# Attention, dense FFN and top-2 MoE on one core: paired score products, a whole fp32 spill, gates first, and late weight conversions

## The chip, the core and the metric

The kernel runs on one core of a Trainium2 chip. Its engines are TensorE (PE in the rows, with PEld for its weight loads), VectorE (DVE), ScalarE (ACT), GpSimd (POOL) and the queue of SyncE (SP), which here only issues transfers; transfers are also issued from POOL. Every instruction stream runs in its own order and waits on semaphores. The metric is the device time of one execution in microseconds, the median of three runs.

## The reference, cut to what is computed

```python
def _attn_ref(q, k, v, f):                       # B 4, H 8, S 576, D 64
    scores = scale * np.matmul(q, k.transpose(0, 1, 3, 2))
    cum = np.cumsum(np.log(np.clip(f, 0.0001, 1.0)), axis=-1)
    decay = cum[:, :, :, None] - cum[:, :, None, :]
    scores = np.where(causal, -1000000000.0, scores + decay)
    scores = scores - np.max(scores, axis=-1, keepdims=True)
    attn = np.exp(scores)
    attn = attn / (np.sum(attn, axis=-1, keepdims=True) + 1e-09)
    return np.matmul(attn, v)
def _moe_ref(x, w_in, w_out):                    # 2304 x 512, d_ff 2048
    h = np.maximum(x @ w_in, 0.0)
    return h * h @ w_out
def _moe2_ref(x, w_gate, w_noise, noise, w1, w2):   # 8 experts, 512 x 1024
    noisy_logits = x @ w_gate + np.log1p(np.exp(x @ w_noise)) * noise
    top2 = ...                                   # two experts a token, softmax of the two
    for e in range(E):
        for k in range(2):
            mask = top2[:, k] == e
            h = np.maximum(x[mask] @ w1[e], 0.0)
            out[mask] += top2_w[mask, k, None] * (h @ w2[e])
```

The three stages follow one another: attention, a dense feed-forward with a squared ReLU, a mixture of eight experts.

## The kernel before, in words

**Arithmetic.** The large products run in float16. A number is kept as a high and a low half, and a product is three matmuls (high by high, high by low, low by high). So each raw float32 weight block `w` of the dense stage (16 blocks, each with a part of w_in and of w_out) must be split once: DVE L550, L555 and L559 make the high half and the rest, ACT L562 and DVE L565 write the two float16 halves. The raw blocks stand in two buffers of the tag "w64"; the last eight are loaded from POOL's queue (L541), and a load waits until the conversion of the block two before it has let its buffer go.

**Attention.** The first 256 positions of each head, the "heads" part, are cut into 12 sub-steps `j`. `hd_s` (L385 on) makes the scores of one sub-step: two PSUM banks, one for each half `z` of 64 partitions; for each half eight float32 products of hraw (L398), two or four products that add the decay (`c`, L403), and two or four that add the causal mask (L409). DVE takes the row maxima (`smh`, L420), ACT the exponentials (`pr`, L431). Sub-steps 0 to 7 stand in an order written out by hand (`PLAN`), with the first weight loads and conversions; sub-steps 8 to 11 run between the steps of the dense stage, in an order that a list scheduler finds. The other 320 positions (`att_*`; scores L226 to L243, products with v L320 and L323) run later, also between steps of the dense stage, from tiles `setk` and `setq` that are prepared from `qkr` loads. The fixed rows of four `setq` tiles are written by POOL (L178 to L180).

**Dense stage.** The tokens go in six chunks of 384. Step `i` of a chunk multiplies with weight block `i`: `mm1` (L585, `m`), ACT and DVE make `r` and `g` (L592 to L603), `mm2` adds into three PSUM tiles `acc` (L647). Chunks 0 and 1 go in two passes of eight blocks each; between them `spill` writes `acc` to memory as two float16 halves (ACT L625, DVE L626), and `unspill` loads them as `bk`, which PE adds to the second pass by twelve products with `ident2k` (L645). `x2_out` writes a finished chunk: `x2`, its transpose `x2T` and its rows `x2d`.

**Experts.** `router` (DVE L728 to L770: `lg` to `mprev`) and `slots` (to `si`, L792) give each token its places in `table`, which POOL writes by scatters (L795). `slot_rows` reads a part of it back (`tix`, L860, and `gs`); `gather` fetches token rows by it (`xg`, L871) and transposes them (`xgT`, SP, L873). `layer1` (L913) and `layer2` (L930) are the two products of an expert, with `hT` between them (ACT L917, DVE L918); POOL adds the result to the output by a scatter (L934). The float32 weights of the experts come through five buffers `wr` (SP, L812 and L816; `fetch_next`), and `split_next` turns one into float16 halves (ACT L835, DVE L836); eight of these make an expert. While chunk 5 runs, the tables of chunk 4 are finished and the rows of expert 0 are gathered.

## Time and profile before

| what | value |
|---|---|
| median of 3 runs | 978.59 us (976.27 to 986.29) |
| profiled execution | 981.3 us, its span 979.1 us |
| PE busy | 944.0 us, 96% of the span |
| DVE, ACT, POOL busy | 570.3, 445.6, 209.4 us |
| mean granted TensorE clock | 0.983 |

The span is the time from the first to the last record of the profiled execution; 2.2 us lie around it. PE is busy nearly all the time, so what can be won is either work that PE does or the few stretches where it waits or runs at the lower clock. The chain that ended last has 71% of its time on PE, 8% on transfers and 5% on DVE.

### The profile page before, as it was taken

To read this page: it belongs to the slowest core of one execution; us is meant where nothing else is said; L and a number is where in the kernel's file an instruction comes from. 1 tells how busy PE (TensorE), PEld (TensorE's weight loads), DVE (VectorE), ACT (ScalarE), POOL (GpSimd) and SP (SyncE) were. 2 spreads that over 40 slices of the span, in tenths; PEclk is the share of its full clock that TensorE was granted. 3 is DMA by queue.
4 is the path that set the end of the run, shared out by engine and by line. 5 is a ranking of instruction groups with operands and counts; after the bars stand their busy time and mean duration, and the time that the engine had idled before them with its cause. 6 is when DMAs were issued, how large, how long until landed. Compare 5 with 4: busy or idle time off the path is not lost.

```text
span 979.1 us, 17623 instructions
## 1 busy us (share of the span) xinstructions
PE 944.0 (96%) x6866; PEld 547.8 (56%) x6866; DVE 570.3 (58%) x1253; ACT 445.6 (46%) x990; POOL 209.4 (21%) x249
## 2 busy tenths in 40 slices
PE   6899989999999999999999899999999999999996
PEld 5766544554555555555555344657474756565662
DVE  6878888777787788776485241525252534334220
ACT  4775758767486566645473110414141323222110
POOL 2000141014041032011002316232232323111102
PEclk7999999999999999999999899999999999999998
DMA  7367858997979949746493914597958484941303
GB/s 301 118 242 224 200 149 267 176 215 172 224 156 250 204 89 234 144 55 99 106 332 113 210 37 97 106 219 174 241 144 188 129 194 96 236 82 27 42 12 43
DMA packets 219879, 155.34 MB, mean 159 GB/s; under 512 B 175698, under 2 KB 186322, under 8 KB 217746
## 3 DMA queue, kind: packets, MB, share of 16 engines
q1 hardware_dynamic: 207234, 124.75, 51.6%
q0 software_dynamic: 12416, 29.31, 14.3%
q8 instruction: 55, 0.90, 0.4%
q10 hardware_dynamic: 144, 0.13, 0.1%
q14 instruction: 30, 0.25, 0.1%
HBM read 89.05 MB, written 23.98 MB: 115 GB/s over the span
## 4 chain that ended last, share of the span: by engine, by line
PE 71%; DMA 8%; issue 7%; DVE 5%; POOL 3%; ACT 2%; SPq 2%; POOLq 0%; DVEq 0%; ACTq 0%
PE e L913 18%; PE e L930 17%; PE m L585 13%; PE acc L647 12%; PE po L320 2%; SPq L873 1%; DMA wr<-in_w_dram 1%; DMA w<-in_w_io_dram 1%; POOL table L795 1%; PE psab L398 1%; PE ps L226 1%; PE ps L227 1%; DMA pt<-phl 1%; PE po L323 1%; DMA xg<-x2d,tix 1%
## 5 line engine op out<-in xcount | busy, mean ns | idle before, releaser
L930 PE MATMUL e<-w2s,hT 128*128 128x512 f16 (+1 forms) x960 | 211.1, 382 | 2.0 <-ACT hT L917 1.3
L913 PE MATMUL e<-xgT,w1s 128*128 128x310 f16 (+2 forms) x1536 | 207.7, 297 | 4.1 <-DMA xgT<-xg 4.1
L647 PE MATMUL acc<-w,g 128*128 128x512 f16 x864 | 205.4, 380 | 0.0
L913 PEld LDWEIGHTS <-w1s 128*128 128x128 f16 x1536 | 140.3, 98 | 70.3 <-issue 8.2
L585 PE MATMUL m<-xT,w 128*128 128x384 f16 x960 | 173.7, 331 | 4.9 <-ACT r L592 3.7
L917 ACT ACTIVATE hT<-e 128x310 f16<-128x310 f32 (+2 forms) x128 | 54.7, 428 | 268.2 <-PE e L913 267.9
L930 PEld LDWEIGHTS <-hT 128*128 128x128 f16 (+1 forms) x960 | 99.8, 104 | 110.1 <-issue 2.2
L585 PEld LDWEIGHTS <-w 128*128 128x128 f16 x1152 | 109.9, 99 | 81.0 <-issue 10.4
L647 PEld LDWEIGHTS <-g 128*128 128x128 f16 x864 | 81.0, 98 | 86.2 <-DVE g L603 0.3
L933 DVE TENSOR_SCALAR y<-e,gs 128x512 f32<-128x512 f32 (+1 forms) x40 | 30.0, 750 | 159.3 <-PE e L930 133.8
L918 DVE SCALAR_TENSOR_TENSOR hT<-e,hT 128x310 f16<-128x310 f32 (+2 forms) x128 | 60.6, 477 | 80.7 <-ACT hT L917 80.4
L934 POOL DMA_INDIRECT out_dram<-y,tix x40 | 65.0, 1625 | 169.6 <-DVE y L933 125.1
L795 POOL DMA_INDIRECT table<-ent,si x36 | 41.4, 1149 | 166.0 <-DVE si L792 156.6
L592 ACT ACTIVATE r<-m 128x384 f32<-128x384 f32 x80 | 39.2, 490 | 68.1 <-PE m L585 67.7
L255 DVE TENSOR_REDUCE sm<-ps 128x1 f32<-128x384 f32 (+2 forms) x96 | 53.1, 562 | 22.1 <-PE ps L243 8.7
L871 POOL DMA_INDIRECT xg<-x2d,tix x40 | 44.3, 1108 | 83.6 <-DMA xgT<-xg 73.3
L258 ACT ACTIVATE pr<-ps,sm 128x384 f32<-128x384 f32 (+1 forms) x64 | 40.2, 630 | 25.8 <-DVE sm L257 23.4
L593 ACT ACTIVATE g<-r 128x384 f16<-128x384 f32 x96 | 50.1, 521 | 3.2 <-PE acc L647 1.5
L836 DVE SCALAR_TENSOR_TENSOR w2s<-wr,w2s 128x1024 f16<-128x1024 f32 x32 | 39.1, 1223 | 19.8 <-ACT w2s L835 19.8
L602 DVE TENSOR_TENSOR r<-r 128x384 f32<-128x384 f32 x64 | 35.4, 553 | 25.2 <-ACT g L593 24.9
L836 DVE SCALAR_TENSOR_TENSOR w1s<-wr,w1s 128x1024 f16<-128x1024 f32 x32 | 39.0, 1225 | 12.7 <-ACT w1s L835 12.5
L279 DVE TENSOR_TENSOR phl<-pr,phl 128x384 f16<-128x384 f32 (+1 forms) x64 | 38.5, 619 | 13.2 <-ACT phl L278 12.8
(281 smaller groups left out, 1085.2 us busy)
## 6 DMA issues: line engine op xcount, KB each, us to landing
wr<-in_w_dram SPq DMA_DIRECT2D x64, 512.0 KB, 5.2
qkr<-in_qk_dram SPq DMA_DIRECT2D x16, 896.0 KB, 6.0
w<-in_w_io_dram SPq DMA_DIRECT2D x8, 1024.0 KB, 4.8
w<-in_w_io_dram POOLq DMA_DIRECT2D x8, 1024.0 KB, 5.7
vr<-in_v_dram SPq DMA_DIRECT2D x16, 320.0 KB, 4.5
x2d<-x SPq DMA_DIRECT2D x18, 256.0 KB, 2.7
hraw<-in_qka_dram SPq DMA_DIRECT2D x8, 512.0 KB, 5.9
out_dram<-zero SPq DMA_DIRECT2D x5, 768.0 KB, 5.2
```

Of the source, the lines that this page charges most:

```text
L255: seen[u] = nc.vector.tensor_reduce(sm[:, z:z + 1], ps[z][:, :N], AX.X, ALU.max).ins
L585: nc.tensor.matmul(ps, W[i][:, wi, 0, 128 * cc:128 * cc + 128], xT[:, xi, cc, r0:r0 + CH], start=(x == 0), stop=(x == 11))
L593: nc.scalar.activation(g[:, 0, :], r, AF.Square, scale=2.0 ** -10)
L647: last[0] = nc.tensor.matmul(acc[t], g[:, gi, 128 * t:128 * t + 128], W[i][:, wi, 1, :], start=(i in ends[c][0] and x == 0), stop=(i in en ...
L795: s_ = nc.gpsimd.indirect_dma_start(out=table, out_offset=bass.IndirectOffsetOnAxis(ap=si[:, t, k:k + 1], axis=0), in_=ent[:, t, k, :], in ...
L836: nc.vector.scalar_tensor_tensor(lo, t_, sc, hi, op0=ALU.mult, op1=ALU.subtract)
L871: nc.gpsimd.indirect_dma_start(out=xg, out_offset=None, in_=x2d[0:seen, :], in_offset=bass.IndirectOffsetOnAxis(ap=rows_t[key, j][0], axis=0))
L913: last[0] = nc.tensor.matmul(ps[:, :hw], w1s[:, cc, wi, 128 * i:128 * i + 128], xgT[:, 4 * xi + cc, c], start=(x == 0), stop=(x == 11)).ins
L917: relu[0] = nc.scalar.activation(hi, ps[:, :hw], AF.Relu).ins
L918: nc.vector.scalar_tensor_tensor(hT[:, i, 1, c], ps[:, :hw], 0.0, hi, op0=ALU.max, op1=ALU.subtract)
L930: last[0] = nc.tensor.matmul(ps[:m], hT[:, i, hi, 128 * j:128 * j + m], w2s[:, i, wi, :], start=(i == 0 and x == 0), stop=(i == NFE - 1 an ...
L934: s_ = nc.gpsimd.indirect_dma_start(out=out, out_offset=bass.IndirectOffsetOnAxis(ap=ix[:m], axis=0), in_=y[:m], in_offset=None, compute_o ...
```

## The change

1. Nine products on a tile of ones stand first on PE (`NWARM`). The load of the gates `fch` is issued from SP as its first transfer, and no longer from ACT.
2. `ident2k` goes. The fixed rows of three of the four `setq` tiles (`make_q`) are written by POOL among the constants at the start.
3. The last block of keys in the 64-row part (`i` of 4) is multiplied with all 128 rows and not with 64; the mask product likewise.
4. `hd_s` issues its products in the order half 0, half 1, half 0, and so on, and for `j` of 8 and more the scheduler may not change that.
5. `spill` writes one float32 sum (ACT alone). `unspill` is one transfer into a buffer of the tag "w64". The twelve products with `ident2k` go; `x2_out` of chunks 0 and 1 adds `bk` on DVE.
6. The first five `wr` loads may be issued only behind the last `x2d` of chunk 4. Of the 16 splits before the experts, eight run in chunk 5, their DVE half behind `si` (L802 in the changed kernel); the other eight run in `layer1` of expert 0, one for each step.
7. `tix` and `gs` have eight buffers and not six.

```diff
-    fch = chain_load(0, HEAD, "pt", 3, nc.scalar)
+    fch = chain_load(0, HEAD, "pt", 3, nc.sync)
+    busy = consts.tile([128, 1], F16, name="busy")
+    nc.vector.memset(busy, 1.0)
+    pw = psX.tile([128, 512], F32, name="pw", tag="xf", bufs=1)
+    for _ in range(NWARM):
+        nc.tensor.matmul(pw, busy.to_broadcast([128, 128]), busy.to_broadcast([128, 512]), start=True, stop=True)
...
+        prev = None
+        for o_, l_, r_, first, end in prods:
+            with ExitStack() as guard:
+                if j >= NPL and prev is not None:
+                    guard.enter_context(tc.issue_after(prev))
+                prev = nc.tensor.matmul(o_, l_, r_, start=first, stop=end, skip_group_check=True).ins
...
-            sp = gpool.tile([128, 2 * DM], F16, name="sp", tag="x2", bufs=3)
-            nc.scalar.activation(sp[:, :DM], acc[t], AF.Copy, scale=2.0 ** -11)
-            nc.vector.scalar_tensor_tensor(sp[:, DM:], acc[t], 2.0 ** -11, sp[:, :DM], op0=ALU.mult, op1=ALU.subtract)
+            sp = gpool.tile([128, DM], F32, name="sp", tag="x2", bufs=3)
+            nc.scalar.activation(sp, acc[t], AF.Copy)
...
+        back[c] = astream.tile([128, NT, DM], F32, name="bk", tag="w64", bufs=2)
+        nc.sync.dma_start(back[c], part[CH * c:CH * c + CH, :].rearrange("(t p) d -> p t d", p=128))
...
-            if i == NA + 4 and c < 2:
-                for z in range(2):
-                    nc.tensor.matmul(acc[t], ident2k, back[t][:, DM * z:DM * z + DM], start=False, stop=False)
...
+            if c < 2:
+                src = back[c][:, t]
+                nc.vector.tensor_tensor(src, acc[t], src, op=ALU.add)
...
-        tix = epool.tile([128, NJ, 2], I32, name="tix", bufs=6)
+        tix = epool.tile([128, NJ, 2], I32, name="tix", bufs=8)
...
+            for n in (0, 1, 3):
+                make_q(n)
...
-            for _ in range(WR):
-                fetch_next()
-        if c == NCH - 1 and i >= 4:
-            split_next()
+            with tc.issue_after(x2_put[0]):
+                for _ in range(WR):
+                    fetch_next()
+        if c == NCH - 1 and 4 <= i < 12:
+            split_next(slotted[0])
...
-    while at["split"] < 16:
-        split_next()
+    def begin(i):
+        split_next(relu[0])
```

How the streams stand. Lines of the changed kernel are some ten higher than those of the kernel before (L385 to L409 there are L392 to L421 here, L550 to L565 are L561 to L576, L812 and L816 are L822 and L826, L860 is L870, L873 is L883).

DVE, kernel before, around the first spill: `w_964` and `w_1073` are the raw and the new tile of weight block 11, `w_991` and `w_1155` those of block 12, `sp` the halves of the spill.

```order
L550 TENSOR_SCALAR w_1073<-w_964 128x1024
L601 TENSOR_TENSOR g<-r,g 128x384
L421 TENSOR_SCALAR smh<-smh 128x2x2
L555 SCALAR_TENSOR_TENSOR w_1073<-w_964,w_1073 128x1024
L420 TENSOR_REDUCE smh<-psab 128x2
L626 SCALAR_TENSOR_TENSOR sp<-acc_699,sp 128x512
L559 SCALAR_TENSOR_TENSOR w_964<-w_964,w_1073 128x1024
L626 SCALAR_TENSOR_TENSOR sp<-acc_703,sp 128x512
L626 SCALAR_TENSOR_TENSOR sp<-acc_707,sp 128x512
L550 TENSOR_SCALAR w_1155<-w_991 128x1024
```

DVE, changed kernel, the same place: the raw tiles of blocks 11 and 12 are `w_983` and `w_1010`.

```order
L561 TENSOR_SCALAR w_1089<-w_983 128x1024
L612 TENSOR_TENSOR g<-r,g 128x384
L566 SCALAR_TENSOR_TENSOR w_1089<-w_983,w_1089 128x1024
L431 TENSOR_REDUCE smh<-psab 128x2 x2
L570 SCALAR_TENSOR_TENSOR w_983<-w_983,w_1089 128x1024
L432 TENSOR_SCALAR smh<-smh 128x2x2
L561 TENSOR_SCALAR w_1171<-w_1010 128x1024
L566 SCALAR_TENSOR_TENSOR w_1171<-w_1010,w_1171 128x1024
L576 SCALAR_TENSOR_TENSOR w_1089<-w_983,w_1089 128x1024
```

The three pieces of the spill are gone, the conversion of block 12 has moved up to that of block 11, and the two maxima of a sub-step stand together.

SP, kernel before, from the last `x2d` of chunk 4 to the first transposes of gathered rows (four more `wr` loads stand ahead of the three `x2T` of that chunk).

```order
L660 DMA x2d<-x_6696 128x1024
L816 DMA wr<-in_w_dram 128x2x512 x4
L812 DMA wr<-in_w_dram 128x1024 x4
L816 DMA wr<-in_w_dram 128x2x512 x4
L812 DMA wr<-in_w_dram 128x1024 x4
L816 DMA wr<-in_w_dram 128x2x512
L860 DMA tix<-table 128x8 x2
L873 DMA_TRANSPOSE xgT<-xg 128x8x128 x8
```

SP, changed kernel, the same place; no `wr` load stands ahead of these rows.

```order
L670 DMA x2d<-x_6685 128x1024
L822 DMA wr<-in_w_dram 128x1024 x4
L826 DMA wr<-in_w_dram 128x2x512 x4
L822 DMA wr<-in_w_dram 128x1024 x4
L870 DMA tix<-table 128x8 x2
L826 DMA wr<-in_w_dram 128x2x512
L883 DMA_TRANSPOSE xgT<-xg 128x8x128 x8
```

Ahead of the two `tix` loads stand 12 `wr` loads, where there were 21, and all of them stand behind chunk 4's `x2d`.

SP, kernel before, the `tix` loads of expert 4 (128x8, then 128x2) among the `wr` loads of expert 3's second layer and expert 4's first.

```order
L860 DMA tix<-table 128x8
L816 DMA wr<-in_w_dram 128x2x512 x2
L860 DMA tix<-table 128x2
L816 DMA wr<-in_w_dram 128x2x512 x2
L812 DMA wr<-in_w_dram 128x1024 x4
```

SP, changed kernel, the same place.

```order
L870 DMA tix<-table 128x8
L826 DMA wr<-in_w_dram 128x2x512
L870 DMA tix<-table 128x2
L826 DMA wr<-in_w_dram 128x2x512 x3
L822 DMA wr<-in_w_dram 128x1024 x4
```

The order is nearly the same there: the second `tix` still stands ahead of `wr` loads, and only the buffer that it needs is another.

## Rows read from the trace of the kernel before

**Rows 1.** Busy time by stretch: PE, PEld, DVE, ACT, POOL; clock, DMA share, GB/s.

```profile
60.00:120.00 60.00, 60.00 (x423) 37.40 (x422) 52.98 (x81) 40.17 (x93) 6.59 (x16) 1.00 0.75 201
140.00:160.00 20.00, 16.34 (x82) 8.26 (x81) 18.13 (x21) 16.00 (x26) 7.75 (x10) 0.91 0.54 179
180.00:200.00 20.00, 20.00 (x186) 11.29 (x184) 16.97 (x36) 16.99 (x40) 0.20 (x1) 1.00 0.87 175
```

**Rows 2.** The chain of waits at the start: start, us, what.

```profile
2.21 8.10 DMA w<-in_w_io_dram
...
15.95 2.01 PE psab L398 x16
```

**Rows 3.** Busy time by stretch, the same columns as rows 1.

```profile
14.00:16.00 2.00, 1.96 (x8) 1.00 (x7) 1.97 (x4) 2.00 (x14) 0.00 (x0) 0.60 0.98 377
...
24.00:26.00 2.00, 2.00 (x23) 1.83 (x23) 0.00 (x0) 1.74 (x6) 0.00 (x0) 0.84 0.97 401
```

**Rows 4.** The chain of waits, sub-step 7 (both halves) and sub-steps after it.

```profile
63.60 1.09 PE psab L398 x16
64.69 0.22 PE psab L403 x4
...
102.14 0.22 PE psab L403 x2
...
103.75 1.09 PE psab L398 x8
...
109.80 0.66 ACT pr L431 x3
```

**Rows 5.** The chain of waits ahead of the load of block 14.

```profile
113.80 15.23 issue
```

**Rows 6.** The timeline of PE: start, us, instruction, idle before it and releaser.

```profile
144.31 3.69 PE L585 MATMUL m<-xT,w 128*128 128x384 f16 x12 [3.26 <-ACT r L592]
```

**Rows 7.** The timelines of DVE and of POOL in the conversions.

```profile
119.33 1.22 DVE L559 SCALAR_TENSOR_TENSOR w<-w,w 128x1024 int32<-128x1024 int32 x1
...
136.72 1.46 DVE L555 SCALAR_TENSOR_TENSOR w<-w,w 128x1024 int32<-128x1024 int32 x1
...
139.31 1.42 POOL L179 TENSOR_SCALAR_AFFINE_SELECT setq<-setq 6x320 f16<-6x320 f16 x1
```

**Rows 8.** The group of one line: duration in ns (least, median, most).

```profile
L626 DVE SCALAR_TENSOR_TENSOR sp<-acc,sp x6: 673/678/683, 99.4 to 147.0; 128x512 f16<-128x512 f32 x6
```

**Rows 9.** The chain of waits in the second pass.

```profile
172.21 0.43 PE acc L645 x2
```

**Rows 10.** The timeline of DVE: the router of chunk 4, and of chunk 5.

```profile
495.87 0.20 DVE L728 TENSOR_SCALAR lg<-pl 128x48 f32<-128x48 f32 x1
...
525.25 0.16 DVE L792 CAST si<-sf 128x6 int32<-128x6 f32 x1
...
571.25 0.20 DVE L728 TENSOR_SCALAR lg<-pl 128x48 f32<-128x48 f32 x1
...
576.41 0.16 DVE L770 TENSOR_TENSOR mprev<-mprev,m__7541 128x8 f16<-128x8 f16 x1
```

**Rows 11.** A line's group on DVE from 485 to 526 us.

```profile
L836 DVE SCALAR_TENSOR_TENSOR w1s<-wr,w1s x8: 1207/1219/1227, 487.3 to 511.9; 128x1024 f16<-128x1024 f32 x8
```

**Rows 12.** The timeline of PE at the start of the experts.

```profile
551.51 6.81 PE L913 MATMUL e<-xgT,w1s 128*128 128x512 f16 x18 [4.11 <-DMA xgT<-xg]
```

**Rows 13.** The timelines of PE and of ACT around 689 us.

```profile
683.01 4.69 PE L930 MATMUL e<-w2s,hT 128*128 128x512 f16 x21
689.02 0.61 PE L930 MATMUL e<-w2s,hT 128*128 128x512 f16 x2 [1.32 <-ACT hT L917]
690.35 10.00 PE L930 MATMUL e<-w2s,hT 128*128 128x512 f16 x38 [0.72 <-DVE hT L918]
...
687.59 1.06 ACT L835 ACTIVATE w2s<-wr 128x1024 f16<-128x1024 f32 x1 [7.13 <-DMA wr<-in_w_dram]
```

**Rows 14.** What SP's queue waited for from 640 to 700 us.

```profile
SPq L860 <- DMA out_dram<-y,tix: 16.4, 2, 15.1
```

More of the change, by code (lines that the diff above doesn't have):

```diff
@@ L167, in decay @@
         return esel[r, u:u + 1].to_broadcast([64, m])
-    ident2k = consts.tile([128, 128], F16, name="ident2k")
     ones16 = consts.tile([128, 128], F16, name="ones16")
@@ L322, in att_pv @@
             else:
-                nc.tensor.matmul(po[64 * h:64 * h + 64, p // 2, 0, p % 2, :], pt[:K, kb, pi, 64 * h:64 * h + 64],
-                                 vs[:K, kb, h, vi, :], start=first, stop=last, skip_group_check=True)
+                nc.tensor.matmul(po[64 * h:64 * h + 64, p // 2, 0, p % 2, :], pt[:, kb, pi, 64 * h:64 * h + 64],
+                                 vs[:, kb, h, vi, :], start=first, stop=last, skip_group_check=True)
         if p == 3:
@@ L391, in hd_s @@
         np_ = 4 // (i + 1)
+        v4 = [t.rearrange("p (c w) -> p c w", w=Wd) for t in ps]
+        prods = []
         for p in range(np_):
@@ L402, in hd_s @@
                 r = slice(64 * z, 64 * z + 64)
-                nc.tensor.matmul(ps[z][:, Wd * p:Wd * p + Wd], decay(r, 4 * b + np_ * a + p, 128), c16[r, 0:Wd],
-                                 start=False, stop=False, skip_group_check=True)
-        v4 = [t.rearrange("p (c w) -> p c w", w=Wd) for t in ps]
+                prods.append((ps[z][:, Wd * p:Wd * p + Wd], decay(r, 4 * b + np_ * a + p, 128), c16[r, 0:Wd], False, False))
         for hf in range(2):
@@ L631, in unspill @@
     def unspill(c):
-        for t in range(NT):
-            if t % 2 == 0:
-                bk = astream.tile([128, 2, 2 * DM], F16, name="bk", tag="pr", bufs=3)
-            back[t] = bk[:, t % 2, :]
-            nc.sync.dma_start(back[t], part[CH * c + 128 * t:CH * c + 128 * t + 128, :])
+        back[c] = astream.tile([128, NT, DM], F32, name="bk", tag="w64", bufs=2)
+        nc.sync.dma_start(back[c], part[CH * c:CH * c + CH, :].rearrange("(t p) d -> p t d", p=128))
     def mm2(c, i):
@@ L1024, in attn_moe_moe_kernel @@
             nc.gpsimd.memset(half[64:128], 1.0)
-            for t_, cmp, val in ((identw, ALU.not_equal, 1.0), (maskw, ALU.is_ge, -BIG), (ident2k, ALU.not_equal, 2048.0)):
+            for t_, cmp, val in ((identw, ALU.not_equal, 1.0), (maskw, ALU.is_ge, -BIG)):
                 nc.gpsimd.memset(t_, 0.0)
-                pin["pool"] = nc.gpsimd.affine_select(t_, t_, [[-1, 128]], cmp, val, base=0, channel_multiplier=1).ins
+                nc.gpsimd.affine_select(t_, t_, [[-1, 128]], cmp, val, base=0, channel_multiplier=1)
+            for n in (0, 1, 3):
+                make_q(n)
         elif tok[0] == "X" and tok[1] != "T":
@@ L1172, in attn_moe_moe_kernel @@
     ov = ctx.enter_context(tc.tile_pool(name="ov", bufs=1, side="left"))
[L1173 to L1174 removed]
     lastp = []
[L1176 removed]
+    def begin(i):
+        split_next(relu[0])
+        if i == NR1:
+            lastp.append(router(NCH - 1, (psE, "e2", 2, 512), last[0]))
+    layer1(0, 0, NE0, begin, last[0])
     layer2(0, 0, NE0, lambda j: slots(NCH - 1, lastp[0], (psE, "e2", 2, 512), last[0]) if j == 0 else None)
```

37 lines of the change are left out of this document (19 added, 18 removed).

## The prediction

> **What bounds the kernel now.** I read the busy time by stretch first, then the chain of waits in the stretches where PE is not full, then the timelines there. PE is busy 60 of 60 us from 60 to 120 us and 20 of 20 from 180 to 200 us at the full clock [rows 1], and it stays so for most of the span: there only work taken from PE counts. Four places are different. (a) Up to 18 us the chain hangs on the first weight block, 8.10 us from issue to landing [rows 2], and behind it PE runs at half clock: 0.60 in the mean from 14 to 16 us and 0.84 from 24 to 26 [rows 3], the two ends of a stretch at 0.50 of full speed, from 14.4 to 24.6 us. (b) From 113.80 us the chain holds 15.23 us that is put down to no wait; it ends where block 14's raw buffer is free and its load can start, 129.0 us [rows 5]. The late conversions push ACT's relu behind them, and PE waits 3.26 us ahead of its products at 144.31 [rows 6]. From 140 to 160 us PE is busy 16.34 us and the clock is 0.91 in the mean [rows 1]: 20 x 0.09 = 1.8 us of PE's time lost to the lower clock. (c) At 547 us PE waits 4.11 us for the rows of expert 0 [rows 12]. (d) At 689 us it waits 1.32 and 0.72 us [rows 13]. The rest of the span gives the change nothing to act on.
>
> **The change part by part.** The sum is made against the profiled execution, 981.3 us.
>
> *Gates first, products on ones: 0, from -5.1 to +1.5.* The weight block ends the start, not the gates, and the transfers ahead of it are the same bytes. The nine products need only a small tile and run while PE would stand idle. What they could give is the clock: in the trace of before it is at half from 14.4 to 24.6 us [rows 3], and the pieces of the chain there are nearly all PE's (16 products of L398 take 2.01 us at 15.95 [rows 2] and 1.09 at 63.60 [rows 4]), so that 10.2 us cost 5.1 us if nothing else bound there. Against it: the new products end before PE's own idle time from 5 to 13 us, in which the real products, if they run faster, leave it idler still. I take 0. The other way, three `make_q` now run on POOL beside the first conversions. Where POOL wrote those rows before, a DVE operation that takes 1.22 us alone took 1.46, and a POOL select 1.42 [rows 7]: 0.24 us for each of some six operations, 1.5 us at most, and the same is given back at 136 us. The Trainium skill (SBUF — State Buffer, Summary: rules for kernel authors) says that a GpSimd operation that reads SBUF beside a VectorE operation with two SBUF inputs fully blocks the later of the two. By that rule the term would be that of the blocked case among the rivals. The rows show DVE stretched by a fifth, not blocked for the whole of a select.
>
> *Alternating halves: PE -6.0.* Eight products of one half take 1.09 us, and sixteen of both halves in turn take the same 1.09; the decay products take 0.22 for two of one half and 0.22 for four of both [rows 4], the mask products likewise. So a half costs 1.53 us, a sub-step in two halves 3.06, in turn 1.53. Four sub-steps (8 to 11) stand in halves: 4 x 1.53 = 6.1 us less on PE. Up to 113 us PE is the bound, so this arrives there in full. Behind it the conversions decide.
>
> *Conversions and spill.* On DVE six operations of 0.68 us [rows 8] leave, 4.1 us in all, two thirds of them ahead of or among the conversions that hold back blocks 14 and 15; six additions, priced by the same rows at the same 4.1, come back at the ends of chunks 0 and 1, where DVE isn't the bound. In the order, block 12's conversion stands right behind block 11's. Counting the moved rows, block 14's load starts between 120 and 123 us in place of 129, and the last conversion ends at 138 to 142 us in place of 148.8. But ACT's relu for step 9 now stands behind the last high half, so PE's wait at 141 us doesn't simply vanish, and the `setk` preparations wait for loads that stand on SP behind the third part of the second spill. `bk` now needs the raw buffers of blocks 14 and 15 and stands on SP ahead of later `qkr` loads; those buffers are free by 142 us, before these loads were issued in the trace of before (151 us on). So of the 6.1 us some may be lost, and of the 3.3 us idle and 1.8 us at the lower clock some may be won. Bounds: -1 (all swallowed by waits for the loads) and -11.2 (6.1 + 3.3 + 1.8). I take -5: nearer to the PE work that is surely gone than to the full recovery.
>
> *No `ident2k`: -2.6.* Twelve products, 0.43 us for two in the chain [rows 9]: 12 x 0.215 = 2.6 us of PE work from 172 to 218 us, where PE is nearly full (180 to 200 us in [rows 1]). The transfer that replaces them moves the same bytes.
>
> *128-row blocks: 0, from -1 to +1.* The 96 products and 16 mask products keep their number and columns; only the rows that they read grow. No row here sets the two apart in a like place.
>
> *Late `wr` loads and splits: -6.9.* In chunk 4's router, `lg` is at 495.87 and `si` at 525.25: 29.4 us. In chunk 5 the same chain goes from `lg` at 571.25 to `mprev` at 576.41 [rows 10], 5.2 us, and needs a few more for the two products and `si`. What fills the difference on DVE is 16 halves of splits (eight of `w1s`, eight of `w2s`) at 1.22 us between its small operations, each held up by ACT and by a `wr` load [rows 11], and the products of the dense stage. With eight of them pinned behind `si` and eight put off, `si` should come at 503 to 507 us. The `tix` loads have 12 `wr` loads ahead and not 21; the first five go at 488 us, the rest as splits free buffers behind `si`, so that the loads reach `tix` at about 517 us, 17 us before 534. PE's wait of 4.11 us at 551.51 then goes, and so does the low clock behind it: 18 products took 6.81 us, 21 warm ones 4.69 [rows 12, 13], so 6.81 - 18 x 0.223 = 2.8 us. Cover: the eight splits of expert 1 stand now beside expert 0's first layer, one for each of its steps of some 3 us, 1.06 us on ACT and 1.22 on DVE, where the hidden tile's own work takes 0.5 and 0.7; there is room. If the last of their `wr` loads come late, ACT holds them and PE waits there instead.
>
> *Eight `tix` buffers: -3.5.* At 682.55 us SP issued the second `tix` of expert 4, after 15.1 us of waiting for a scatter that still read the old buffer [rows 14]; the `wr` loads behind it came late, ACT's split waited 7.13 us for one, and the relu behind that split made PE wait 1.32 + 0.72 us and then run 38 products in 10.00 us, where the row above has 0.223 each [rows 13]: 1.5 us more. With eight buffers the new tile takes that of expert 1's first blocks, which is read out some 20 us sooner. 1.32 + 0.72 + 1.5 = 3.5.
>
> Sum: 0 - 5 - 2.6 + 0 - 6.9 - 3.5 = -18.0; 981.3 - 18.0 = 963.3 us for an execution like the profiled one. That execution stands 0.28% above the median of 978.59, so the median should be 963.3 x 0.9972 = 960.6, say **961 us**.
>
> **The rivals.**
>
> *The attention's gain is swallowed.* The set preparations wait for loads and conversions whatever PE saves ahead of them; of -5 there is -1, and the handover gives its idle time only (-4.1). For it: the chain from 113 to 165 us holds little of PE. Against it: block 14's load waits for DVE work that the change takes away or moves up. -1 - 2.6 - 4.1 - 3.5 = -11.2; 970.1, as a median 967.
>
> *Full recovery and a warm start.* Stalls and cold products at 144 us go altogether (-11.2) and the clock stays up from 14 us on (half of 5.1, since DVE's maxima hold some of that stretch): -11.2 - 2.6 - 2.6 - 6.9 - 3.5 = -26.8; 954.5, as a median 952.
>
> *The handover doesn't move.* The pin does what it says but `si` stays late, since the dense stage's own DVE work holds up the router. Then expert 0's eight splits come late too: -18 + 6.9 = -11.1, 970.2, median 967 to 968.
>
> *The first conversions are blocked.* If each of those six operations stood for a whole select at the 1.42 us of [rows 7], the chain behind the first weight block grows by 6 x 1.42 = 8.5 us: 963.3 + 8.5 = 971.8, median 969. Against it stand the 1.46 us of the same rows, and that the selects are over by some 13 us. This is how the rule cited above would show.
>
> *Slower: both banks at once.* The second product of a sub-step now needs its second PSUM bank at once, not some 10 us later, and PE stands in order. A bank is free when ACT's exponentials have read it: those of the half issued at 103.75 us ended at 110.46 [rows 4], 5.4 us after that half's last product. If PE waited 5.4 us in each of the four sub-steps, 21.6 us are lost against a gain of 18.0: 984.9, median 982. It decides from 4.5 us a sub-step on. Against it: the scheduler put the first product of a sub-step alone ahead of a run of `m` products, and three banks stand for two.
>
> **How the numbers follow.** My forecast has 0.55, the swallowed gain 0.14, the full recovery 0.12, the fixed handover 0.12, the blocked conversions 0.03, the slower case 0.04. The forecast's own range, from the bounds of the attention's term and of the start, goes from 953 to 968 as a median; with the cases on either side 948 to 973 should hold 8 in 10. About 1% is what a measurement of this kernel can tell from no change: 968.8 and 988.4. Faster by more: the forecast and the full recovery, and most of the two cases at 967, 0.84. Within: 0.12, most of it the blocked case and what lies above 967 of those two. Slower by more: 0.04, with what I don't see.
>
> **What would show it.** L421 in the changed kernel: 16 products in about 1.1 us between 60 and 115 us, no piece of 8 in 1.1. Block 14's load issued before 124 us and the last conversion over by 142. No product with `ident2k`. `si` of chunk 4 before 508 us, `tix` before 520, and PE at 547 us with a wait under 0.5 us and the clock at 1.00. No wait of PE at 680 to 692 us, and no `tix` waiting on `out_dram` there. The clock between 14 and 25 us tells whether the products on ones did anything. The forecast is wrong if PE's idle time between 113 and 165 us grows by as much as its work has shrunk, if waits for `psab` banks appear on PE, or if ACT waits for `wr` in expert 0's first layer.

## The result, and the profile after

| what | before | changed |
|---|---|---|
| median, 15 runs each in turn | 978.03 us (971.64 to 986.29) | 969.48 us (965.51 to 976.60) |
| profiled execution | 981.3 us, span 979.1 us | 968.64 us, span 966.8 us |
| mean granted clock | 0.983 | 0.989 |

The ratio is 0.9914, with an interval from 0.9893 to 0.9935: 8.4 us faster (6.4 to 10.5). The forecast was 17 us.

One point in the program divides the gain. The last `acc` product of the dense stage ends at 547.40 us before (541.41 + 5.99, the row below) and at 544.59 now (538.60 + 5.99, further down): 2.8 us, where the prediction had 7.6 (attention 5, `ident2k` 2.6). From there to the end of the span it was 431.7 us and is 422.2: 9.5 us, where the prediction had 10.4.

```profile
541.41 5.99 PE L647 MATMUL acc<-w,g 128*128 128x512 f16 x27
```

The second of these readings is steady, the first is not. Behind the last `acc` product the five traced executions without part 6 took 430.1 to 434.9 us and the fifteen with it 420.2 to 427.1. The point itself varies by several us for one and the same program: four executions whose first half is that of the kernel before (before, b_late, b_tix8, b_late_tix8_y6) reach it between 547.4 and 553.0 us, four with that of the changed kernel (itself, a_again, a_again2, a_y6) between 542.3 and 545.8. The means are 7.5 us apart, but the first four executions lie 3.3 to 7.6 us above the medians of their kernels, 5.4 on average, and the other four 1.0 below on average. With these distances taken off, about 1 us is left, an estimate from these eight executions. The medians say the same: 8.4 us were gained in all and some 9.5 behind this point. So the second half of the kernel did nearly what was forecast, and the first half gave little or nothing of its 7.6 us.

In the second half, first DVE's router of chunk 4 in the changed kernel, to be read beside [rows 10]: `si` now follows `lg` by 12.6 us, where it was 29.4.

```profile
490.05 0.21 DVE L738 TENSOR_SCALAR lg<-pl 128x48 f32<-128x48 f32 x1 [0.53 <-PE pl L734]
...
502.67 0.17 DVE L802 CAST si<-sf 128x6 int32<-128x6 f32 x1
```

PE at the start of the experts in the changed kernel, beside [rows 12]: 72 products without a wait ahead of them, at 0.218 us each, where 18 had taken 6.81 us behind a wait of 4.11.

```profile
538.60 5.99 PE L651 MATMUL acc<-w,g 128*128 128x512 f16 x27
544.42 15.70 PE L923 MATMUL e<-xgT,w1s 128*128 128x512 f16 x72
```

SP issued the two `tix` loads at 518.18 us (534.47 before). Around 689 us, where [rows 13] had two waits, PE is now full, but two small waits stand earlier, and from 560 to 680 us it misses 1.4 us. The changed kernel's stretches by busy time (columns as in rows 1), and then its PE timeline:

```profile
60.00:120.00 60.00, 51.94 (x357) 30.20 (x355) 49.15 (x74) 38.49 (x87) 4.91 (x16) 0.96 0.80 211
120.00:140.00 20.00, 19.86 (x146) 11.91 (x147) 15.27 (x23) 10.15 (x22) 3.10 (x5) 0.85 0.73 173
140.00:165.00 25.00, 22.54 (x145) 12.27 (x144) 19.39 (x26) 19.98 (x36) 4.56 (x8) 1.00 0.70 238
560.00:680.00 120.00, 118.64 (x809) 67.70 (x808) 53.79 (x129) 36.12 (x65) 43.73 (x42) 1.00 0.71 162
680.00:700.00 20.00, 20.00 (x94) 9.75 (x93) 3.95 (x5) 0.00 (x0) 8.53 (x8) 1.00 0.92 211
```

```profile
643.20 5.34 PE L940 MATMUL e<-w2s,hT 128*108 128x512 f16 x24 [0.43 <-DVE y L943]
657.38 17.58 PE L923 MATMUL e<-xgT,w1s 128*128 128x310 f16 x132 [0.94 <-DVE hT L928]
```

Now the first half, by the first three of those stretches. From 60 to 120 us PE was busy for all of 60 us [rows 1]; now it is busy for 51.94, and its clock falls to 0.85 in the next stretch. The halves do alternate (14 products in 1.16 us at 74.21, 13 in 1.04 at 104.97). But PE stands for transposes. Its group of the products with v of sub-steps 8 to 11, from 60 to 165 us (busy us, mean ns, idle before it, and what ended that), in the kernel before and in the changed one:

```profile
L515 PE MATMUL po<-vh,pt 128*128 128x64 f16 x96 | 4.0, 194 | 0.9 <-DMA pt<-phl 0.9
```

```profile
L526 PE MATMUL po<-vh,pt 128*128 128x64 f16 x96 | 4.7, 208 | 8.2 <-DMA pt<-phl 8.2
```

The wait grew from 0.9 us to 8.2, and all of PE's idle time in this window from 5.5 to 10.7. `pt` is the transpose of the attention weights `phl`, issued on SP. The changed kernel's chain of waits goes through two of them:

```profile
90.82 8.55 DMA pt<-phl
...
107.24 12.85 DMA pt<-phl
```

ACT begins to prepare the remaining 320 positions (`setk`) once the weight blocks are nearly all converted. First the kernel before, then the changed one:

```profile
147.47 1.15 ACT L196 ACTIVATE setk<-qkr 128x1152 f16<-128x1152 f32 x1
```

```profile
147.92 1.15 ACT L204 ACTIVATE setk<-qkr 128x1152 f16<-128x1152 f32 x1
```

PE has less work up to there, and in this pair the point has not moved. From POOL's first weight load to it the four executions with the first half of before took 79.4 to 83.7 us, 82.0 on average, and the four with that of the changed kernel 79.0 to 82.2, 80.5 on average: 1.5 us for the whole of attention's work up to there.

Between lie POOL's loads of blocks 14 and 15, before and changed:

```profile
129.05 0.53 POOL L541 DMA_DIRECT2D w<-in_w_io_dram  x1 [14.94 <-DVE w L565]
132.62 0.53 POOL L541 DMA_DIRECT2D w<-in_w_io_dram  x1 [3.05 <-DVE w L565]
```

```profile
120.76 0.53 POOL L552 DMA_DIRECT2D w<-in_w_io_dram  x1 [11.60 <-DVE w L576]
132.19 0.53 POOL L552 DMA_DIRECT2D w<-in_w_io_dram  x1 [10.90 <-DVE w L576]
```

Block 14's load moved as the prediction had it (120 to 123 us), block 15's did not move, and the last conversion ends at 145.5 us, where 138 to 142 was forecast and 148.8 was before.

At the start, PE in the changed kernel and its clock, beside [rows 2, 3]:

```profile
1.00 4.02 PE L133 MATMUL pw<-busy 128*128 128x512 f16 x9 [1.00 <-DVE busy L130]
5.06 1.84 PE L421 MATMUL psab<-hraw 64*128 64x128 f32 x16
...
13.80 2.48 PE L448 MATMUL psfl<-identf,pr 128*128 128x128 f32 x7 [4.71 <-ACT pr L442]
```

```profile
14.00:16.00 2.00, 2.00 (x7) 1.09 (x6) 1.97 (x5) 2.00 (x14) 0.00 (x0) 0.50 1.00 391
...
24.00:26.00 2.00, 2.00 (x32) 1.48 (x30) 0.00 (x0) 1.59 (x9) 0.00 (x0) 1.00 0.84 319
```

The scores of the first sub-steps are done by some 9 us and not 12, but the first operation on a weight block comes at 11.01 us (10.33 before). PE waits 4.71 us in between and its clock then falls to half. That is earlier than before, and it is over by 20 us in place of 25. What this gives is gone further on: POOL's first weight load (block 8), a point that all traced executions share, comes at 64.9 to 70.5 us in the seven without part 1 and at 65.0 to 71.9 in the thirteen with it.

One correction to the words on the kernel before: the raw weight blocks are 64-bit words, which the integer operations L550 to L559 turn into float32 before the two halves are split off. Their buffers and their order are as described.

### The profile page after: what moved, and what is told of

It is laid out like the page before. It is cut to its first block, busy times and chain, and to the rows that moved or that the text cites. A ratio compares the mean times of both kernels' runs of the same rounds, so it can differ in the third digit from the quotient of the medians.

```text
span 966.8 us, 17599 instructions
## 1 busy us (share of the span) xinstructions
PE 930.4 (96%) x6863; PEld 539.9 (56%) x6863; DVE 568.7 (59%) x1254; ACT 446.5 (46%) x990; POOL 201.4 (21%) x247
## 4 chain that ended last, share of the span: by engine, by line
PE 79%; DMA 11%; DVE 4%; issue 3%; ACT 1%; SPq 1%; POOL 0%; DVEq 0%; POOLq 0%; ACTq 0%
PE e L923 20%; PE e L940 18%; PE acc L651 15%; PE m L596 13%; DMA pt<-phl 6%; PE m1s L596 3%; PE po L327 2%; PE psab L421 2%; DMA vr<-in_v_dram 1%; DMA out_dram<-y,tix 1%; PE ps L234 1%; PE ps L235 1%; DMA w<-in_w_io_dram 1%; PE po L330 1%; DMA xgT<-xg 1%
## 5 line engine op out<-in xcount | busy, mean ns | idle before, releaser
L923 PE MATMUL e<-xgT,w1s 128*128 128x310 f16 (+2 forms) x1536 | 204.9, 294 | 0.9 <-DVE hT L928 0.9
L596 PE MATMUL m<-xT,w 128*128 128x384 f16 x960 | 171.0, 327 | 3.8 <-ACT r L603 2.6
L881 POOL DMA_INDIRECT xg<-x2d,tix x40 | 41.3, 1033 | 128.1 <-DMA xgT<-xg 121.0
L846 DVE SCALAR_TENSOR_TENSOR w2s<-wr,w2s 128x1024 f16<-128x1024 f32 x32 | 39.1, 1222 | 17.1 <-ACT w2s L845 15.2
L845 ACT ACTIVATE w2s<-wr 128x1024 f16<-128x1024 f32 x32 | 33.6, 1052 | 26.1 <-DMA wr<-in_w_dram 25.4
```

The source lines that it names most:

```text
L596: nc.tensor.matmul(ps, W[i][:, wi, 0, 128 * cc:128 * cc + 128], xT[:, xi, cc, r0:r0 + CH], start=(x == 0), stop=(x == 11))
L881: nc.gpsimd.indirect_dma_start(out=xg, out_offset=None, in_=x2d[0:seen, :], in_offset=bass.IndirectOffsetOnAxis(ap=rows_t[key, j][0], axis=0))
L923: last[0] = nc.tensor.matmul(ps[:, :hw], w1s[:, cc, wi, 128 * i:128 * i + 128], xgT[:, 4 * xi + cc, c], start=(x == 0), stop=(x == 11)).ins
```

## The experiments

Names with `b_` are the kernel before with an edit, those with `a_` the changed kernel with an edit. Kernels of one batch ran on the same chip beside the same runs of the kernel before. Times are medians; us from a ratio are worked out against 978.

### First batch: one part at a time

The sum of the prediction has four terms. Theory one: each part brings its term. Theory two: what attention saves is taken back by waits.

**b_halves**: only part 4 (alternating halves).

```diff
...
-                    nc.tensor.matmul(ps[z][:, c], hd["x", b, i][r, 1, pp, :], hd["x", b, kb][r, 0, pp, :], ...)
+                    prods.append((ps[z][:, c], hd["x", b, i][r, 1, pp, :], hd["x", b, kb][r, 0, pp, :], p == 0 and kb == 0, False))
...
+                if j >= NPL and prev is not None:
+                    guard.enter_context(tc.issue_after(prev))
...
```

> The kernel before with part 4 alone (products of the two halves in turn, kept so for sub-steps 8 to 11). Theory 1, swallowed: PE loses about 6 us of work up to 113 us, but PE then stands for the transposed tiles pt of the sub-steps, so by 165 us nothing is left: 0 to -2.5 us against the kernel before, and waits of PE on pt of 4 us or more between 90 and 125 us. Theory 2, the prediction's term: -5 us, and no such waits.

Measured: 981.06 us against 981.72, ratio 0.9985 (0.9954 to 1.0016), which is 1.5 us less, with an interval from 4.5 less to 1.6 more. The groups of PE from 60 to 165 us show what it saved and where it waits. Kernel before, then b_halves:

```profile
L585 PE MATMUL m<-xT,w 128*128 128x384 f16 x226 | 41.6, 335 | 3.7 <-ACT r L592 3.7
...
L398 PE MATMUL psab<-hraw 64*128 64x128 f32 x80 | 10.3, 284 | 0.0
...
L403 PE MATMUL psab<-c,esel 64*128 64x256 f16 x20 | 3.5, 272 | 0.0
L409 PE MATMUL psab<-masku,identb 64*128 64x256 bf16 x20 | 3.3, 270 | 0.0
```

```profile
L589 PE MATMUL m<-xT,w 128*128 128x384 f16 x227 | 41.7, 335 | 4.4 <-ACT r L596 4.4
...
L414 PE MATMUL psab<-hraw 64*128 64x128 f32 x80 | 7.9, 291 | 0.0
L519 PE MATMUL po<-vh,pt 128*128 128x64 f16 x96 | 4.2, 205 | 3.6 <-DMA pt<-phl 3.6
...
L414 PE MATMUL psab<-masku,identb 64*128 64x256 bf16 x20 | 2.7, 270 | 0.0
L414 PE MATMUL psab<-c,esel 64*128 64x256 f16 x20 | 2.6, 270 | 0.0
```

The same 120 products take 17.1 us in halves and 13.2 in turn: 3.9 us less (the prediction had 6.1). The waits for `pt` grew from 0.9 to 3.6 us and those for `r` from 3.7 to 4.4: 3.4 us come back. Theory two holds here: 5 us lies outside the interval. The profiled execution of b_halves lies 7.9 us above its median, so the shares come from an unusually long one.

**b_late**: only part 6.

```diff
-            for _ in range(WR):
-                fetch_next()
-        if c == NCH - 1 and i >= 4:
-            split_next()
+            with tc.issue_after(x2_put[0]):
+                for _ in range(WR):
+                    fetch_next()
+        if c == NCH - 1 and 4 <= i < 12:
+            split_next(slotted[0])
...
```

> The kernel before with part 6 alone (late wr loads, splits behind si or in layer1). Both theories: the wait of 4.1 us for xgT and the low clock behind it go, -6.9 us in the stretch from 480 to 560 us, si before 508 us. Rival: the handover's gain is smaller than its rows, because what is late next (wr, or the splits in layer1) makes PE wait: -3 us or less.

Measured: 971.52 us, ratio 0.9885 (0.9838 to 0.9932), which is 11.2 us less (6.7 to 15.8). `si` stands 13.0 us behind `lg`, and PE in b_late goes over to the experts without a wait:

```profile
546.96 5.99 PE L647 MATMUL acc<-w,g 128*128 128x512 f16 x27
552.78 15.70 PE L915 MATMUL e<-xgT,w1s 128*128 128x512 f16 x72
```

From the end of the last `acc` product to the end of the span it takes 424.3 us in place of 431.7: 7.4 us, against a term of 6.9.

**b_tix8**: only part 7 (`bufs=6` to `bufs=8` for `tix` and `gs`).

> The kernel before with part 7 alone (eight buffers for tix and gs). Prediction's term: -3.5 us, no wait of PE from 680 to 692 us. Rival: the stall at 689 us has another release, the wr loads themselves, and stays: 0 to -1 us.

Measured: 981.25 us, ratio 0.9984 (0.9954 to 1.0014), which is 1.6 us less, with an interval from 4.5 less to 1.4 more: the term of 3.5 is neither shown nor excluded by the time. PE is full from 680 to 700 us, and a new wait stands 28 us earlier. PE, POOL, DVE and a piece of the chain of waits in b_tix8:

```profile
660.98 7.03 PE L930 MATMUL e<-w2s,hT 128*108 128x512 f16 x24 [2.48 <-DVE y L933]
```

```profile
646.26 0.95 POOL L871 DMA_INDIRECT xg<-x2d,tix  x1 [5.12 <-DMA xgT<-xg]
647.66 0.95 POOL L871 DMA_INDIRECT xg<-x2d,tix  x1 [0.46 <-issue]
648.92 2.67 POOL L934 DMA_INDIRECT out_dram<-y,tix  x1 [0.31 <-issue]
```

```profile
660.17 0.75 DVE L933 TENSOR_SCALAR y<-e,gs 128x512 f32<-128x512 f32 x1 [10.11 <-DMA out_dram<-y,tix]
```

```profile
648.92 11.12 DMA out_dram<-y,tix
```

With the new buffers the last rows of expert 3 and those of expert 4 are gathered earlier. On POOL's queue four gathers of expert 3 now stand between the start of a `y` and its scatter to the output, one of them after a wait of 5.12 us for its `xg` buffer; in the kernel before there were three, with one wait of 3.19. So the scatter is issued 10.1 us after its `y` was begun, where it was 6.7, and it lands 11.12 us later. `y` has three buffers, so DVE waits for that landing before it can write the next one, and PE waits 2.48 us for DVE. The 24 products behind it take 7.03 us, where 24 x 0.223 = 5.35. So 2.48 + 1.7 = 4.2 us go where 3.5 were won. This execution, too, is a long one, 5.8 us above its median.

**a_nohalves**: the changed kernel with the score products half after half.

> The changed kernel with part 4 undone (halves one after the other, in the scheduler's own order). Theory 1, swallowed: as fast as the changed kernel, within 1.5 us of it (about 968 to 971), PE's waits for pt before 125 us shorter by as much as its work is longer. Theory 2: 5 us slower than the changed kernel, about 974 to 975.

Measured: 971.17 us, ratio 0.9866 (0.9812 to 0.9919). No loss without the alternating halves. Its trace shows the exchange of work for waiting from the other side: from 60 to 165 us PE is idle for 5.8 us, where it is 10.7 in the changed kernel, and the wait for `pt` is 2.5 us and not 8.2.

```profile
L522 PE MATMUL po<-vh,pt 128*128 128x64 f16 x96 | 4.0, 193 | 2.5 <-DMA pt<-phl 2.5
```

### Second batch: which wait takes attention's place, and what `y` costs

**a_again**: the changed kernel as it is.

> The changed kernel once more, to stand beside the others on the same chip: 0.991 of the kernel before.

Measured: 970.15 us against 977.23, ratio 0.9932 (0.9901 to 0.9963).

**a_lag3**: the products with v of a sub-step one dense step later, to give `pt` more time.

```diff
-        if NPL <= j - 2 < NSUB:
-            hd_pv16(j - 2)
+        if NPL <= j - 3 < NSUB:
+            hd_pv16(j - 3)
...
```

> The changed kernel with the products with v of sub-steps 8 to 11 one step of the dense stage later, so that the transposed tiles pt have some 10 us more. Theory 1, swallowed by pt: PE's waits for pt before 145 us fall from 8.2 to under 1.5 us, the clock stays up, and the time is 3 to 6 us below the changed kernel's. Rival: what comes behind (the last conversions, the set preparations and their loads up to 165 us) decides alone; the waits for pt go and the time stays within 1.5 us.

Measured: 971.51 us, ratio 0.9937 (0.9909 to 0.9965), and 8.8 us of waits for `pt`. The scheduler moved the products forward again, so this run doesn't tell the theories apart.

**a_y6**: six `y` buffers in place of three, which leaves the order of every engine as it is.

> The changed kernel with six buffers for y, not three; no other instruction moves. Theory: the eight tix buffers only moved the stall at 689 us to 640 to 665 us, where gathers that wait for a transpose stand on POOL ahead of the scatters that free y. Then PE's waits on DVE y and hT from 560 to 700 us (1.3 us, and what the clock adds) go, and the time falls by 1 to 3 us. Rival: those waits are of one execution only, 0 us.

Measured: 968.17 us, ratio 0.9888 (0.9848 to 0.9928): 2.0 us below a_again by the medians, 4.3 by the ratios, with overlapping intervals. The wait for `y` is gone; a wait of 0.60 us for `hT` remains at 680 us.

**b_late_tix8_y6**: the kernel before with parts 6 and 7 and six `y` buffers, and nothing of attention.

> The kernel before with part 6, part 7 and six buffers for y: nothing else of the change. If the attention's parts (start, halves, spill) are worth nothing together, it is as fast as the changed kernel or up to 4 us faster (0.985 to 0.991 of the kernel before). If they are worth the 7.6 us of the prediction, it is 4 us or more slower than the changed kernel.

Measured: 972.71 us, ratio 0.9925 (0.9898 to 0.9952). Beside a_y6, which has parts 1 to 5 more, it is 4.5 us slower by the medians, 3.6 by the ratios with overlapping intervals. The prediction had 7.6 for these parts, 2.6 of them for `ident2k`. If `ident2k` gave its 2.6, which no run shows by itself, 1 to 2 us are left of attention's 5; the intervals are too wide to exclude the 7.6 by this pair alone.

### Third batch: the small transfers ahead of the transposes

On SP the second `pt` stands behind the load of the router's weights (`wgr`) and the first writes of `table`. Theory: these hold it back.

**a_setup**: all of them behind the last `pt`; **b_setup**: the same in the kernel before; **a_setup_y6** and **a_nohalves_setup_y6**: with six `y` buffers, the latter also without alternating halves.

```diff
...
-        if (n, i) == (1, 1):
-            with tc.issue_after(pin["sp"]), tc.issue_after(pin["pool"]):
-                router_setup()
+        if j == NSUB:
+            with tc.issue_after(pin["turn"]):
+                router_setup()
```

Here `pin["turn"]` is the issue of the last `pt`.

> The changed kernel with the router's set-up (the load of its weights, the small writes that fill the table) issued behind the last transposed tile pt of the sub-steps, not between them. Theory 1b: the gain of the halves was lost because the second pt tile stands on SP behind the table's small writes and its weights' conversion stands ahead of it on ACT; then that tile's issue takes under 5 us on SP, PE's waits for pt before 145 us fall from 8 us to under 3, and the time falls by 3 to 6 us, to 0.985 to 0.989 of the kernel before. Rival: the waits for pt go but the last conversions and the set preparations decide: within 1.5 us of the changed kernel.

> The kernel before with the router's set-up moved in the same way and nothing else. PE is full from 60 to 120 us there in any case, so 0 to -2 us by both theories.

> The same with six buffers for y: 1 to 3 us less than that, 0.983 to 0.987 of the kernel before, no wait of PE on y or hT from 640 to 700 us.

> The same without part 4 (halves one after the other). Theory 1b: 4 to 6 us slower than with the halves in turn. Rival, the halves are worth nothing whatever stands behind them: within 1.5 us.

Measured, against 979.28: a_setup 968.55 (ratio 0.9907, 0.9873 to 0.9942); b_setup 976.83 (0.9979, 0.9950 to 1.0008); a_setup_y6 966.77 (0.9883, 0.9847 to 0.9918); a_nohalves_setup_y6 973.87 (0.9961, 0.9930 to 0.9993). PE in a_setup, from 60 to 165 us:

```profile
L651 PE MATMUL acc<-w,g 128*128 128x512 f16 x165 | 41.5, 393 | 2.9 <-ACT sp L636 2.0 <-DVE g L612 0.9
...
L526 PE MATMUL po<-vh,pt 128*128 128x64 f16 x96 | 4.7, 200 | 3.6 <-DMA pt<-phl 3.6
```

The issue of the second `pt` on SP takes 3.5 us there in place of 10.8, as the theory had it, and the waits for `pt` fall to 3.6 us, but others come up (for `sp` 2.0, `g` 0.9, more for `r`), and PE is idle for 10.4 us there, as it was for 10.7. The wait that the change brought was removed in good part, and the time stayed. The `pt` wait is where the gain went in the trace, not what holds it.

Six `y` buffers gave 1.8 us here (a_setup_y6 against a_setup), again with overlapping intervals. Without alternating halves the kernel lost 7.1 us here, which contradicts a_nohalves.

### Last six: the loop of the weight blocks

Weight blocks 8 to 15 come through two raw buffers: load, five operations on DVE and ACT, then the load of the block after next. In the changed kernel the stretch from POOL's first of these loads to the first `setk` takes 82.2 us (79.4 before), and 77 to 84 in all runs told so far, whether PE has more work there or less. Theory: this loop sets the end. In the order DVE's first operation for a block, which waits for its load, stands ahead of the low half of the block before it, which lets a buffer go.

**a_order**: that first operation behind the low half, for blocks from 10 on; **b_order**: the same in the kernel before; **a_order_y6** and **a_order_setup_y6**: with the earlier edits.

```diff
+            if i >= 10:
+                guard.enter_context(tc.issue_after(wlast[0]))
+            conv_shift(i)
-        for part_ in (conv_shift, conv_top, conv_rest, conv_high, conv_low):
+        for part_ in (conv_top, conv_rest, conv_high, conv_low):
```

> The changed kernel with one thing more: DVE begins the conversion of a weight block from 10 on only behind the low half of the block before it, so that the low half, which lets the raw buffer go, no longer stands behind a wait for the next block's load. Theory: attention's end is set by the loop of load, conversion and load of the late weight blocks through two raw buffers, and not by PE. Then the stretch from POOL's first weight load to ACT's first setk shortens by 2 to 5 us from the 80 to 82 that it has in the changed kernel, and the time falls by 2 to 5 us, to a ratio of 0.986 to 0.989. Rival, the transposes pt on SP's queue set it: the weight loads come earlier but the waits for pt stay, and the time stays within 1.5 us of the changed kernel run beside it.

> The changed kernel as it is, beside the other three on the same chip: a ratio of 0.990 to 0.993. It is the foot for them, and with the one without alternating halves it gives that part's worth inside the whole change.

> The changed kernel with the score products of a sub-step half after half, as in the kernel before; run before at 0.987 on another chip. Theory that alternating is worth nothing, since waits take its place: within 2 us of the changed kernel beside it. Rival, that the PE work that it saves (5 us) arrives at least in part: 3 to 6 us slower than the changed kernel. Third, that alternating costs (it asks for both banks at once): 3 us faster or more, as its first run against the other chip's median would have it.

> All that was found together: the changed kernel with the conversions of late blocks in order, the router's small writes behind the last pt, and six y buffers. The last two alone gave 966.8, a ratio of 0.988. If the loop of the weight blocks binds, 962 to 965, a ratio of 0.983 to 0.986; if not, 966 to 968.

Measured on one chip, against 981.79: a_order 967.31 (ratio 0.9872, 0.9828 to 0.9916); a_again2 971.11 (0.9897, 0.9858 to 0.9936); a_nohalves2 970.60 (0.9887, 0.9847 to 0.9928); a_order_setup_y6 972.56 (0.9905, 0.9870 to 0.9940). a_order looks like what the theory said: 3.8 us below a_again2 by the medians, 2.4 by the ratios with overlapping intervals, and a stretch to `setk` of 75.6 us. But a_order_setup_y6, which has that edit and two more, is 5.3 us above a_order, and its stretch is 81.4. Without alternating halves the changed kernel is 0.5 us faster here, and again it works more and waits less: PE is idle for 6.9 us from 60 to 165 us, where it is 9.0 in a_again2.

> The kernel before with this alone: DVE begins the conversion of a weight block from 10 on only behind the low half of the block before it. If the loop of load and conversion of the late blocks sets attention's end whatever PE's work is, the loads of blocks 12 to 15 come every 8 to 9 us in place of 107.5, 113.6, 129.0 and 132.6, the stretch from POOL's first weight load to ACT's first setk shortens by some 4 us from 79.4, and the time falls by 2 to 5 us, a ratio of 0.995 to 0.998. Rival, PE's work is the bound in the kernel before and only the changed kernel has the room: ratio 0.999 to 1.002 and PE as full as before from 60 to 113 us.

> The changed kernel with the conversions of late blocks in order and six y buffers, without the pinned small writes. Theory: both gains of the single runs (3.8 us beside the changed kernel on the same chip, and about 2) add up: 2 to 3 us under the run with the order alone, a ratio of 0.983 to 0.987. Rival, that the order's gain was chance of the schedule and of the run: 0.987 to 0.991, with the loads of the late blocks uneven again.

Measured, against 979.70: b_order 976.84 (0.9955, 0.9928 to 0.9982); a_order_y6 968.43 (0.9887, 0.9853 to 0.9920). b_order is faster by 4.4 us, but its loads are as uneven as ever (104.68, 117.16, 126.89, 133.26 us) and the stretch to `setk` is 78.9, so its gain isn't shown to come from the loop. a_order_y6 gained nothing over a_y6 (0.9888), and its stretch is 82.8.

a_order and a_order_y6 have the same instructions in the same order on every engine. They differ in the `y` buffers alone, which come into use after 550 us. So their first 150 us are two executions of one program. a_order, ACT and then POOL's loads of blocks 12 and 13:

```profile
102.35 0.26 ACT L690 ACTIVATE wg<-wgr 128x64 f16<-128x64 f32 x1 [1.09 <-DMA wgr<-in_wgn_dram]
...
141.19 1.16 ACT L204 ACTIVATE setk<-qkr 128x1152 f16<-128x1152 f32 x1
```

```profile
100.58 0.53 POOL L552 DMA_DIRECT2D w<-in_w_io_dram  x1 [7.71 <-DVE w L576]
109.28 0.55 POOL L552 DMA_DIRECT2D w<-in_w_io_dram  x1 [6.33 <-DVE w L576]
```

a_order_y6, the same:

```profile
109.00 0.26 ACT L690 ACTIVATE wg<-wgr 128x64 f16<-128x64 f32 x1 [6.99 <-DMA wgr<-in_wgn_dram]
...
149.25 1.16 ACT L204 ACTIVATE setk<-qkr 128x1152 f16<-128x1152 f32 x1
```

```profile
101.34 0.53 POOL L552 DMA_DIRECT2D w<-in_w_io_dram  x1 [7.62 <-DVE w L576]
115.72 0.55 POOL L552 DMA_DIRECT2D w<-in_w_io_dram  x1 [11.11 <-DVE w L576]
```

SP issued `wgr`, a load of 64 columns, at 100.68 us in the one and at 102.45 in the other. ACT could use it 1.7 us later in the one and 6.6 in the other. Behind it on ACT stand `phl`, which the next transpose needs, and the high half of a weight block (105.73 and 112.28 us), behind which the low half and the next load wait. Of the 8.1 us between the two `setk`, 0.9 was there at the first load, and 5 to 6 came from this one wait. In the changed kernel the same wait was 1.74 us.

## Why the prediction was wrong, point by point

**The step that failed** is "Up to 113 us PE is the bound, so this arrives there in full", and with it the attention term of -5. PE was full there, but the chain through ACT, SP and DVE to the last converted block lay close beneath it. As soon as PE had less to do, PE waited for `pt` (8.2 us, 0.9 before), and the stretch from the first weight load to the first `setk` stayed at some 80 us. Part 4 alone, for which the prediction had 6.1 us of PE's work, gave 1.5 us, and at most 4.5. Of the 7.6 us for attention and `ident2k` together one pair of profiles shows 2.8 at the last `acc`, eight executions set against their medians about 1, and a_y6 beside b_late_tix8_y6 some 4. Of the other half of the term, the conversions, block 14's load came at 120.76 us as forecast, but block 15's stayed where it was, and the last conversion ended 3.4 us earlier and not 7 to 11.

The term's low bound, -1, and the rival of the swallowed gain had this mechanism, with a chance of 0.14. That its time, 967, is 2.5 us from the result is in part luck: it had the handover at 4.1 where 6.9 came, and the `tix` buffers at 3.5 where no gain is shown, and the two nearly cancel. The 969 of the blocked conversions fits the number alone: nothing of its mechanism is in the trace.

The term was also mis-sized in itself: a sub-step in halves was priced from pieces of the chain at 3.06 us against 1.53. Counted by the groups of b_halves, four sub-steps gave 3.9 us and not 6.1.

**The eight `tix` buffers** were a second, smaller failure. The mechanism was right, and the wait at 689 us went, but what is late next was not asked. A gather that comes earlier stands ahead of a scatter that frees `y`: b_tix8's trace shows 4.2 us given back for 3.5, and its time no gain clear of the noise. Six `y` buffers gave 2.0 and 1.8 us in two pairs, with overlapping intervals.

**The handover** was right in place, mechanism and size: `si` at 502.67 us (forecast 503 to 507), `tix` at 518.18 (about 517), no wait of PE, full clock; b_late's tail is shorter by 7.4 us for a term of 6.9, and no tail with part 6 is as long as the shortest without it. The rival in which it doesn't move fell.

**The start** at 0 was right, and for the reason given: the weight block ends it, and PE, done earlier, waited longer. The rival of blocked conversions fell: POOL's last select ended at 12.4 us, the conversions' 1.22 us are unchanged. What was stretched was a select, 0.86 us in place of 0.45, beside DVE's first two operations. By the rule of the Trainium skill that the prediction weighed (SBUF — State Buffer, Summary: rules for kernel authors), an operation of DVE with two SBUF inputs would be blocked beside a select that began first; the first such operation of the conversions began at 13.01 us, when the selects were over, so the changed kernel doesn't test it at this place. The prediction read [rows 7] as speaking against the rule, and they hardly do. The DVE operation of 1.46 us began when 0.38 us of a select were left, and it grew by 0.24; the select of 1.42 us began 0.35 us into a DVE operation, where one alone takes 0.45 in the changed kernel. So 1.42 us was also too high a price for a select in that rival.

**Both banks at once**: PE's waits from 60 to 165 us are 8.2 for `pt`, 1.9 for `r` and 0.6 for `pr`, none for a bank. The 5.4 us of that rival were misread: the exponentials that ended at 110.46 us belong to the sub-step whose halves were issued at 96.34 and 101.06, and those of the half issued at 103.75 began at 119.34.

**`ident2k` and the 128-row blocks** had no run of their own; the twelve products are gone from the trace.

**The base.** The sum was made against one execution of 981.3 us and then scaled by 0.28%. The changed kernel's profiled execution is 5.3 us above the 963.3 forecast for one like it, nearly all ahead of the handover. The other 3.6 us of the miss at the median come from the base: the step from that execution to the median took 2.7 us off, and the changed kernel's execution stands 0.8 below its own median.

**What stays open.** Which of the coupled waits ends attention in most executions isn't settled. Moving the small transfers took away most of the wait for `pt`, and putting the conversions in order evened the late loads in one execution of three; neither moved the time in every pair. What alternating halves are worth inside the whole stays open as well: without them the kernel was 0.5 us faster beside a_again2 and 7.1 slower beside a_setup_y6. An earlier `wgr` load, which the last pair points to, was not tried, nor a third raw buffer. No version is shown to beat the changed kernel: a_setup_y6 (0.9883), a_y6 (0.9888) and a_order (0.9872) have lower ratios, with intervals that reach into its own.

## What to carry to other kernels

A full engine is the bound only up to the length of the next chain beneath it: before work taken from it is counted as time, follow the other queues to the same point and see how much later they would be. When a buffer is added so that something starts earlier, look at what stands behind that thing on its queue. And a sum that is made against one profiled execution carries that execution's own luck, here up to 8 us of 980, so a term of that size has to be read from medians of many runs, and a point in the trace from several executions.

## What was not expected of the hardware

One small load, in the same order of instructions, took 1.7 us in one execution and 6.6 in another until it could be used, and 5 to 6 of the 8.1 us by which the end of attention moved came from it. The issue of the second `pt` transpose held SP's queue for 1.3 us in the kernel before and for 10.8 in the changed one; with the same program up to there it was 10.3 us in a_again, 11.0 in a_y6 and 4.4 in a_again2. In a_setup, where neither `wgr` nor the writes of `table` stood ahead of it, it was 3.5. The nine products on ones ran at half rate themselves, 0.447 us each where one of 512 columns takes 0.218 later. Behind them the two groups of 16 score products took 1.84 and 1.05 us, where they took 2.08 and 1.77 before. The clock stood at 0.50 from 14 to 16 us, after 4.7 us in which PE waited.
